# Delta-rule attention with a causal mixture on one core: small products on four array places, masks on other engines, a new order

## The chip, the cores and the metric

The kernel runs on one core of a Trainium2 chip. The metric is the device time of one execution in microseconds; the median of three runs stands for the kernel. TensorE (PE) multiplies, VectorE (DVE), ScalarE (ACT) and GpSimd (POOL) do the rest (POOL works on SBUF alone here), and all loads and stores are issued on SyncE's queue (SP).

## What is computed

The first half is linear attention with a delta rule over 4 batches, 8 heads, 768 tokens and 48 features; the second half is causal attention with four experts of 64 features, mixed by a top-2 gate.

```python
for t in range(S):
    y[:, :, t] = einsum('bhd,bhde->bhe', q[:, :, t], state)
    v_old = einsum('bhde,bhd->bhe', state, k_n[:, :, t])
    state = state + b[:, :, t] * einsum('bhd,bhe->bhde', k_n[:, :, t], v[:, :, t] - v_old)
x = y.transpose(0, 2, 1, 3).reshape(B, S, H * D)
for e in range(E):
    q, k, v = x @ wq[e], x @ wk[e], x @ wv[e]
    a = softmax(causal(q @ k.T / 8))
    out += gate[e] * (a @ v @ wo[e])
```

## The kernel before, in words

The work is cut into six units (`n`): two batches and 256 tokens each, that is 16 sequences of (batch, head), kept as 8 pairs (`p`) of two (`f`). A unit has four chunks (`c`) of 64 tokens. The features of sequence f lie on partitions 0 to 47 or 64 to 111 (`feat(f)`); its tokens lie on the opposite half (`tok(f)`), so a product from features to tokens uses one off-diagonal corner of TensorE's array for f = 0 and the other for f = 1.

Per chunk: `ga` forms k k^T and `gp` k q^T (16 small products each, two instructions a product); `pm` masks the latter on DVE. Then the state passes through: `ks` (state times keys), `xs` (v minus that, DVE), `tx` (times the solved triangular matrix in GF), `us` (copies, DVE and ACT), `ku` (adds to the state in PSUM bank 0), `se` (copies the state back), and `yy` gives the outputs; `yh`, `yl` and the small DMAs `hx` bring them into the layout of the second half, split in a high and a low part.

```python
def ga(n, c):
    g, k = slots(("ga", n, c), NP, 64), KF[zi(n, c) % RK]
    for p in range(NP):
        for f in range(2):
            mm(g[tok(f), p], k[feat(f), p], k[feat(f), p])
```

Once per unit the triangular system is solved for all 32 (chunk, pair): `bi` transposes on DVE, `nm` takes the norms by Newton steps, `sv.0` to `sv.32` eliminate in 32 steps (`sv.1` to `sv.30` are two POOL instructions each, one behind the other; `sv.31` is a selection on POOL), `bo` and `tn` transpose back on DVE, and `m1`, `we`, `m2`, `me` combine the two 32-token halves. Unit 0 has a solve of its own: `s0` on DVE in steps of 16 tokens, then `p1`, `w1`, `p2`, `w2`. POOL also scales v (`vs`) when its tile has landed.

The second half of a unit: `pj` and `pv` project, `kh`, `kl`, `ve` copy; `mx` forms scores for the row maximum, with a mask added by two bf16 products at the end; `mr` reduces on DVE; `mt`, `mo` turn the maximum; `sc` forms the scores again, transposed, in two banks; `sm` adds the mask there on DVE; `ex` takes the exponential on ACT; `av` multiplies with v on 128 rows and two column halves; `oe`, `ra`, `rb`, `nr` normalise (the last on POOL), `ft`, `oh`, `ol`, `fo`, `oo`, `so` project and store. `gt` is the gate.

PSUM has eight banks; bank 0 holds the state. The order of all 1711 steps is written out by hand as a string, ORDER: each word is a step with its numbers, and what stands behind @ is the bank, or the banks, of its result. Each engine executes its instructions in that order. `fl.31@2` issues 31 filler products of zeros, 128 columns each, whose result nobody reads.

Of the kernel before, what the change touches and what calls it, by code (L numbers as in the profile page):

```python
# [20 lines left out]
NEG = -1.0e9  # L21
RK, RQ, RV, RA = 8, 5, 3, 3
# [8 lines left out]
pm.0.0.1 ga.0.1@5 am.2 ae.3.2 ae.3.1 ae.3.0 ae.3.3 sq.1 al.3.3 ae.1.1 fl.3@6 gp.0.3@1 ae.1.2 ae.1.3 am.3 ae.1.0 sr.1
al.1.3 ga.1.0@2 am.1 pm.0.3.1 al.3.1 al.1.1 pm.0.3.0 gp.1.0@3 ge.1.0 bi.0 gp.0.1@1 sq.3 sq.2 fl.7@6 gp.0.2@2 sr.3 sr.2
ga.1.2@4 nm.0.0 nm.0.1 ga.1.1@5 ge.1.2 nm.0.2 wh.0 ge.1.1 nm.0.3 fl.10@6 ga.1.3@4 nm.0.4 ci bs ge.1.3 s0.1 s0.2 gd.1
s0.3 ww.1 s0.4 s0.5 s0.6 s0.7 s0.8 s0.9 s0.10 s0.11 s0.12 s0.13 s0.14 s0.15 wh.1 bi.1 wl.0 vs.0.1 ww.2 nm.1.0 vs.0.0
tn.0 wl.1 wh.2 bo.0 vs.0.2 ww.3 wl.2 nm.1.1 fl.208@6 p1.0@4 zz.3 ww.4 p1.3@5 nm.1.2 wh.3 wl.3 p1.1@6 w1.0 nm.1.3 wh.4
p1.2@4 wl.4 ww.5 p2.0@7 w1.1 w1.2 nm.1.4 ww.6 p2.2@4 sv.1.0 wh.5 p2.1@6 wl.5 w2.0.0 w2.2.0 wh.6 w2.0.1 tc0.0.1 w1.3
tc0.0.0 sv.1.1 w2.0.2 tc0.2.0 m1.0.2@5 sv.1.2 w2.2.2 tc0.2.1 m1.0.0@7 sv.1.3 w2.1.0 we.0.2 pm.0.2.0 sv.1.4 tc0.1.0
p2.3@5 pm.1.0.1 tc0.1.1 cl.0.0.1 we.0.0 cl.0.0.0 pm.1.0.0 sv.1.5 m2.0.0@7 pm.0.1.0 sv.1.6 m1.0.1@3 w2.3.1 me.0.0.0
w2.3.2 me.0.0.1 cl.0.1.0 w2.3.0 we.0.1 sv.1.7 tx.0.0@7 pm.0.1.1 tc0.3.1 tc0.3.0 w2.2.1 sv.1.8 m1.0.3@3 lv.0.3 us.0.0.0
us.0.0.1 ga.2.0@1 we.0.3 w2.1.2 sv.1.9 w2.1.1 ku.0.0 pm.0.2.1 ge.2.0 sv.1.10 yy.0.0@3 se.0.0.1 lt.0.3 se.0.0.0  # L40
m2.0.1@1 lq.1.1 sv.1.11 yh.0.0.0 ks.0.1@2 me.0.1.0 yl.0.0.0 me.0.1.1 cl.0.1.1 m2.0.2@4 yh.0.0.1 xs.0.1 lk.2.1 sv.1.12
m2.0.3@1 me.0.2.0 yl.0.0.1 lv.1.0 tx.0.1@5 me.0.2.1 me.0.3.0 sv.1.13 me.0.3.1 gp.1.1@4 us.0.1.0 us.0.1.1 cl.0.2.0
ku.0.1 pm.1.1.0 cl.0.3.1 sv.1.14 yy.0.1@1 pm.1.1.1 se.0.1.0 lt.1.0 se.0.1.1 ga.2.1@2 cl.0.2.1 lq.1.2 yh.0.1.0 sv.1.15
yh.0.1.1 ks.0.2@3 yl.0.1.0 ge.2.1 yl.0.1.1 cl.0.3.0 hx.0.0 xs.0.2 sv.1.16 lk.2.2 fl.11@7 tx.0.2@1 lv.1.1 sv.1.17
gp.1.2@2 us.0.2.1 us.0.2.0 yy.0.2@1 sv.1.18 pm.1.2.1 pm.1.2.0 ku.0.2 yh.0.2.0 lq.1.3 sv.1.19 ga.2.2@3 yl.0.2.0
se.0.2.0 lt.1.1 se.0.2.1 sv.1.20 pj.0.3.0.0@2 ge.2.2 pj.0.1.0.0@4 yh.0.2.1 pj.0.1.0.1 sv.1.21 pj.0.0.0.0@3 yl.0.2.1
pj.0.2.0.0@5 pj.0.3.0.1 ks.0.3@1 vs.0.3 sv.1.22 pj.0.2.0.1 xs.0.3 lk.2.3 pv.0.0.1@6 lv.1.2 sv.1.23 pj.0.0.0.1 ve.0.0.1
# [24 lines left out]
nm.3.4 oh.0.0 m1.2.1@4 kh.1.3.2 ol.0.0 me.2.0.0 pj.1.2.2.2 cz.2 kl.1.3.2 we.2.1 pv.1.1.0@7 kh.1.2.2 sv.3.0 m2.2.1@3
ve.1.1.0 lg.1.1.0 kl.1.2.2 sv.3.1 mx.1.0.1.1@45 sv.3.2 me.2.1.1 pm.3.0.0 fo.0.0.1@6 sv.3.3 me.2.1.0 pm.3.0.1 sv.3.4
# [761 lines left out]
```

## Time and profile before

| | |
|---|---|
| median of three runs (lowest, highest) | 489.33 us (488.55, 490.82) |
| profiled execution, span | 490.0 us |
| PE busy | 468.3 us, 96% |
| DVE, ACT, POOL busy | 282.3, 196.1, 217.7 us (58%, 40%, 44%) |
| instructions | 22373, of them 10076 products |
| filler products (zb) | 432, 29.2 us busy |
| HBM read, written | 21.92 MB, 4.72 MB |

Busy time of TensorE counts from the start of a product to its modelled end, and products overlap; so 96% does not say that the array is full. Two things are better guides: the distance from one block's start to the next one's start, and the idle time with what ended it. The profiled execution takes its time from the first to the last instruction; the runs' times stand 0.7 us lower at the median.

### The profile page before, as it was taken

To read this page: it belongs to the slowest core of one execution; us is meant where nothing else is said; L and a number is where in the kernel's file an instruction comes from. 1 tells how busy PE (TensorE), PEld (TensorE's weight loads), DVE (VectorE), ACT (ScalarE), POOL (GpSimd) and SP (SyncE) were. 2 spreads that over 40 slices of the span, in tenths; PEclk is the share of its full clock that TensorE was granted. 3 is DMA by queue.
4 is the path that set the end of the run, shared out by engine and by line. 5 is a ranking of instruction groups with operands and counts; after the bars stand their busy time and mean duration, and the time that the engine had idled before them with its cause. 6 is when DMAs were issued, how large, how long until landed. Compare 5 with 4: busy or idle time off the path is not lost.

```text
span 490.0 us, 22373 instructions
## 1 busy us (share of the span) xinstructions
PE 468.3 (96%) x10076; PEld 412.6 (84%) x10076; DVE 282.3 (58%) x561; ACT 196.1 (40%) x393; POOL 217.7 (44%) x416
## 2 busy tenths in 40 slices
PE   9995799899999999998999999999999999999997
PEld 8895698798889888887888899988988778877896
DVE  3899544195665777639457787414862375148511
ACT  4231244133445154444353344533545344442553
POOL 3243378812888248860386832897300110011111
PEclk9588559899999999999799999999999999999999
DMA  8832023342332523333113343201422011000101
GB/s 210 246 70 67 4 54 87 104 103 51 103 85 74 103 50 101 82 92 78 24 50 94 111 107 65 52 18 43 112 58 66 3 50 35 17 1 33 35 3 66
DMA packets 52863, 34.37 MB, mean 70 GB/s; under 512 B 34816, under 2 KB 46848, under 8 KB 52768
## 3 DMA queue, kind: packets, MB, share of 16 engines
q1 hardware_dynamic: 52768, 32.95, 25.8%
q8 instruction: 79, 1.29, 1.2%
q14 instruction: 16, 0.13, 0.1%
HBM read 21.92 MB, written 4.72 MB: 54 GB/s over the span
## 4 chain that ended last, share of the span: by engine, by line
PE 85%; DVE 8%; issue 3%; DMA 2%; ACT 1%; SPq 1%; ACTq 0%
PE p L183 82%; PE p L749 1%; DVE tm L404 1%; DVE vs L406 1%; DMA kf<-in_kq_dram 1%; PE p L675 1%; DVE tn L415 1%; DMA xu<-h 1%; SPq L575 1%; DVE b L471 1%; DVE qp L334 1%; DVE at L342 1%; DVE gf L412 0%; DMA qp<-in_kq_dram 0%; DVE ss L363 0%
## 5 line engine op out<-in xcount | busy, mean ns | idle before, releaser
L465 POOL TENSOR_TENSOR tm<-b 128x30 f32<-128x30 f32 (+9 forms) x150 | 72.8, 485 | 34.5 <-DVE rs L736 14.3
L467 POOL TENSOR_TENSOR b<-b,tm 128x30 f32<-128x30 f32 (+9 forms) x150 | 77.7, 518 | 11.8
L711 ACT ACTIVATE at<-p 128x768 f32<-128x768 f32 (+1 forms) x48 | 43.4, 916 | 34.7 <-PE p L183 21.5
L185 ACT ACTIVATE z<-p 48x384 f32<-48x384 f32 (+1 forms) x68 | 33.0, 486 | 45.5 <-PE p L183 40.7
L666 DVE TENSOR_REDUCE mp<-p 128x2 f32<-128x1024 f32 (+3 forms) x40 | 44.2, 1115 | 11.1 <-PE p L183 10.6
L183 PE MATMUL p<-vs,at 128*64 128x65 f32 x1344 | 47.2, 224 | 0.6 <-issue 0.6
L183 PEld LDWEIGHTS p<-vs,at 128*64 128x64 f32 x1344 | 42.3, 137 | 6.4 <-issue 3.4
L511 POOL TENSOR_TENSOR kv<-kv,nt 128x384 f32<-128x384 f32 x24 | 19.8, 831 | 60.8 <-DMA kv<-in_kv_dram 60.8
L183 PE MATMUL p<-xu,wh 128*128 128x512 f32 (+1 forms) x168 | 43.6, 399 | 0.3 <-DMA xu<-h 0.3
L334 DVE TENSOR_TENSOR qp<-p,cs 64x512 f32<-64x512 f32 x48 | 32.9, 688 | 8.6 <-PE p L183 7.9
L183 PEld LDWEIGHTS p<-xu,wh 128*128 128x128 f32 x168 | 30.1, 209 | 6.8 <-DMA xu<-h 0.5
L742 POOL TENSOR_TENSOR rs<-rs,gw 128x8 f32<-128x8 f32 x12 | 3.3, 278 | 71.8 <-DVE rs L739 71.6
L183 PE MATMUL p<-kf 48*64 48x64 f32 x768 | 31.6, 243 | 2.5 <-DMA kf<-in_kq_dram 2.5
L183 PE MATMUL p<-qp,kf 48*64 48x64 f32 x768 | 30.7, 232 | 2.7 <-issue 1.0
L183 PEld LDWEIGHTS p<-kf 48*64 48x64 f32 x768 | 28.7, 156 | 5.4 <-DMA kf<-in_kq_dram 2.7
L183 PEld LDWEIGHTS p<-qp,kf 48*64 48x64 f32 x768 | 27.4, 146 | 4.9 <-issue 2.2
L183 PE MATMUL p<-qh,kh 64*128 64x128 f32 (+1 forms) x192 | 30.9, 318 | 0.0
L183 PE MATMUL p<-zb 128*128 128x128 bf16 x432 | 29.2, 229 | 1.1 <-DVE zb L298 1.1
L533 DVE COPY z<-p 64x384 f32<-64x384 f32 x24 | 13.5, 561 | 26.5 <-ACT z L185 21.4
L183 PEld LDWEIGHTS <-zb 128*128 128x128 bf16 x432 | 26.6, 103 | 2.0 <-DVE zb L298 1.1
L183 PE MATMUL p<-qp,z 128*48 128x64 f32 (+1 forms) x768 | 27.2, 225 | 0.0
L183 PE MATMUL p<-qh,kl 64*128 64x128 f32 (+1 forms) x192 | 27.1, 278 | 0.0
(143 smaller groups left out, 991.0 us busy)
## 6 DMA issues: line engine op xcount, KB each, us to landing
kv<-in_kv_dram SPq DMA_DIRECT2D x46, 192.0 KB, 2.8
kf<-in_kq_dram SPq DMA_DIRECT2D x24, 224.0 KB, 3.1
out_dram<-ot SPq DMA_DIRECT2D x24, 192.0 KB, 2.3
qp<-in_kq_dram SPq DMA_DIRECT2D x38, 96.0 KB, 2.4
gf<-gf SPq DMA_DIRECT2D x20, 128.0 KB, 2.9
xu<-h SPq DMA_DIRECT2D x72, 32.0 KB, 2.1
qp<-in_kq_dram SPq DMA_DIRECT2D x10, 128.0 KB, 5.7
gf<-zr SPq DMA_DIRECT2D x10, 128.0 KB, 3.2
```

The costliest lines, as they stand in the source:

```text
L183: T.matmul(o, lhsT=a, rhs=b, start=start, stop=True, skip_group_check=True)
L185: copy = lambda o, a: S.activation(o, a, AF.Copy)
L334: V.tensor_tensor(QP[zi(n, c) % RQ][r, f], slots(("gp", n, c), NP, 64)[r], PMK[r, None, :].to_broadcast([64, NP, 64]), op=OP.mult)
L342: V.tensor_copy(o, a)
L404: V.tensor_tensor(tv, BX[:, :, i:i + 1, i + 1:].to_broadcast([128, 2, i, m]), BX[:, :, 0:i, i:i + 1].to_broadcast([128, 2, i, m]), op=OP.mult)
L406: V.tensor_tensor(BX[:, :, 0:i, i + 1:], BX[:, :, 0:i, i + 1:], tv, op=OP.add)
L465: G.tensor_tensor(tv, B2[:, i:i + 1, i + 1:].to_broadcast([128, i, m]), B2[:, 0:i, i:i + 1].to_broadcast([128, i, m]), op=OP.mult)
L467: G.tensor_tensor(B2[:, 0:i, i + 1:], B2[:, 0:i, i + 1:], tv, op=OP.add)
L511: G.tensor_tensor(vt, vt, NRM[n % 2][:, c * NP:c * NP + NP, None].to_broadcast([128, NP, HD]), op=OP.mult)
L533: V.tensor_copy(o, a)
L666: V.tensor_reduce(o[:, :, y0:y0 + per], g, axis=AX.X, op=OP.max, negate=True)
L711: S.activation(at(n, b, y, kp)[:, :, 0:w], P8[:, b0:b0 + 2, 0:w], AF.Exp, scale=0.125)
```

## The change

The step `l3` and the bf16 mask tiles go. Every odd pair of units 1 to 5 now keeps its tokens on the same half as its features (`rows`), and even pairs as before; the host lays out v and beta accordingly. `ga`, `ks` and `tx` then go round the four corners of the array, and where ORDER gives them two neighbouring banks (20 of 24 `ga`, 19 of 22 `ks`, 20 of 24 `tx`) even pairs write the one and odd pairs the other (`duo`). The mask of `mx` becomes a DVE addition in PSUM (`mk`, 32 of them) between `mx` and `mr`; `sm` becomes a selection on POOL behind `ex`. There are six instead of five buffers for q, four instead of three for k and v by token, five instead of three for the exponentials, which ORDER now assigns. Filler products have 512 columns; there are 51 of them instead of 432. ORDER is new throughout.

```diff
-RK, RQ, RV, RA = 8, 5, 3, 3
+RK, RQ, RV, RA = 8, 6, 4, 5
-zb zz.2 lk.0.2 lk.0.0 lt.0.0 lq.0.0 lc.0 ex0 lk.0.3 lk.0.1 lt.0.1 zz.1 lq.0.3 lk.1.0 lq.1.0 lq.0.1 l3 lt.0.2 lq.0.2
+zb fl.1@1 fl.1@2 fl.1@3 fl.1@4 fl.1@5 fl.1@6 fl.1@7 lt.0.1 sq.1 lt.0.3 sq.3 lt.0.2 sr.1 lt.0.0 lk.0.3 sq.2 sr.2 sq.0
...
+def rows(n, p, f):
+    g = f if n and p % 2 else 1 - f
+    return slice(64 * g, 64 * g + 64)
...
+    def two(key, w):
+        a, b = BK[key]
+        return P8[:, a:b + 1, 0:w]
...
+    def duo(key, w):
+        b = BK[key]
+        if len(b) == 1:
+            return slots(key, NP, w).rearrange("p (k t) w -> p k t w", t=2)
+        return two(key, 4 * w).rearrange("p t (k w) -> p k t w", w=w)
...
-    ZB = sb("zb", 128, dt=BF16)
-    IB = sb("ib", 128, dt=BF16)
-    MB = sb("mb", 128, dt=BF16)
+    ZB = sb("zb", 512, dt=BF16)
...
-            mm(P8[:, BK["fl", k][0], 0:128], ZB, ZB)
+            mm(P8[:, BK["fl", k][0]], ZB[:, 0:128], ZB)
...
-        g, k = slots(("ga", n, c), NP, 64), KF[zi(n, c) % RK]
+        g, k = duo(("ga", n, c), 64), KF[zi(n, c) % RK]
         for p in range(NP):
             for f in range(2):
-                mm(g[tok(f), p], k[feat(f), p], k[feat(f), p])
+                mm(g[rows(n, p, f), p // 2, p % 2], k[feat(f), p], k[feat(f), p])
...
-                mm(g[tok(f), p], k[feat(f), p], z[feat(f), f, p])
+                mm(g[rows(n, p, f), p // 2, p % 2], k[feat(f), p], z[feat(f), f, p])
...
-                mm(g[tok(f), p], GF[n % 2][tok(f), NP * c + p], x[tok(f), p])
+                mm(g[tok(f), p // 2, p % 2], GF[n % 2][rows(n, p, f), NP * c + p], x[rows(n, p, f), p])
...
-        if k0 + nb == 2 * (n % 3) + i + 1:
-            for x in range(2):
-                mm(g[:, x, :, 128 * nb - 128:], IB, MB[:, None, :].to_broadcast([128, per, 128]), False)
+
+    def mk(n, b, i, r):
+        k0, nb, y0, per, sec, g = mv(n, b, i, r)
+        V.tensor_tensor(g[:, :, :, 128 * nb - 128:], g[:, :, :, 128 * nb - 128:], KM[:, None, None, :].to_broadcast([128, 2, per, 128]),
+                        op=OP.add)
...
-        b0 = BK["sc", n, b, y, n % 3][0]
-        g = P8[:, b0:b0 + 2, 0:256].rearrange("p x (j q) -> p x j q", j=2)
-        V.tensor_tensor(g, g, KM[:, None, None, :].to_broadcast([128, 2, 2, 128]), op=OP.add)
+        a = at(n, b, y, n % 3)[:, :, 0:256].rearrange("p x (j q) -> p x j q", j=2)
+        G.affine_select(a, a, pattern=[[0, 2], [0, 2], [1, 128]], compare_op=OP.is_ge, fill=0.0, base=0, channel_multiplier=-1)
```

The first place is the start on DVE, around the transposition of unit 0's matrix (`vs<-tn`) and the scaling that follows (`vs<-vs,aa`, two instructions). Before, up to the first Newton step (the other thirteen norm instructions, up to aa, stand behind these, and then the scaling):

```order
L334 TENSOR_TENSOR qp_75<-p_63,cs 64x512 x2
L392 STREAM_TRANSPOSE vs<-tn 128x1024
L363 TENSOR_REDUCE ss_86<-vs 128x8 x2
L371 TENSOR_SCALAR g_87<-ss_86 128x32
L372 TENSOR_SCALAR g_87<-g_87 128x32
L374 RECIPROCAL rr_88<-g_87 128x32
```

And now:

```order
L357 COPY at_111<-p_63 32x256
L396 TENSOR_SCALAR nt_98<-g_89 128x32
L397 TENSOR_TENSOR rr_90<-nt_98 128x32
L398 RECIPROCAL rr_90<-rr_90 128x32
L399 STREAM_TRANSPOSE nn_91<-rr_90 128x32
L400 TENSOR_TENSOR aa_92<-nn_91,bt 128x32
L404 STREAM_TRANSPOSE vs<-tn 128x1024
L409 SCALAR_TENSOR_TENSOR vs<-vs,aa_92 128x16x16 x2
```

The sums (ss) and the whole norm moved ahead of the transposition, and the masking of q (qp) went away from the copies.

The second place is DVE behind the small solve of unit 0, where `gf<-vs` is the transposition that releases p1 on PE, `b<-gf` unit 1's first, and `tn<-vs` the one that p2 needs. Before:

```order
L408 TENSOR_TENSOR vs<-vs,aa_90 128x2x16x16
L409 COPY vs<-aa_90 128x32
L392 STREAM_TRANSPOSE b<-gf_81 128x1024
L370 COPY ss_91<-b 128x32
L371 TENSOR_SCALAR g_92<-ss_91 128x32
L372 TENSOR_SCALAR g_92<-g_92 128x32
L415 STREAM_TRANSPOSE tn<-vs 128x32x32
L412 STREAM_TRANSPOSE gf_80<-vs 128x32x32
```

And now:

```order
L420 TENSOR_TENSOR vs<-vs,aa_92 128x2x16x16
L421 COPY vs<-aa_92 128x32
L424 STREAM_TRANSPOSE gf_82<-vs 128x32x32
L404 STREAM_TRANSPOSE b<-gf_83 128x1024
L427 STREAM_TRANSPOSE tn<-vs 128x32x32
L382 COPY ss_93<-b 128x32
```

The releasing transposition moved from the third of three to the first.

The third place is POOL inside the solve of unit 3, where `tm<-b` and `b<-b,tm` are the solve's steps, `at` holds exponentials, and rs and os are a normalisation. Now:

```order
L479 TENSOR_TENSOR b<-b,tm 128x18x13
L720 AFFINE_SELECT at_111<-at_111 128x2x256
L746 TENSOR_TENSOR rs_119<-rs_119,gw_132 128x8
L747 TENSOR_TENSOR os_117<-os_117,rs_119 128x512
L477 TENSOR_TENSOR tm<-b 128x228
L479 TENSOR_TENSOR b<-b,tm 128x19x12
```

A selection and a normalisation stand in the queue between two steps of the solve; before, no selection of exponentials stood on POOL at all.

## Rows read from the trace of the kernel before

**Rows 1.** Page, chain of waits: shares of the span by line.
```profile
PE p L183 82%; PE p L749 1%; DVE tm L404 1%; DVE vs L406 1%; DMA kf<-in_kq_dram 1%; PE p L675 1%; DVE tn L415 1%; DMA xu<-h 1%; SPq L575 1%; DVE b L471 1%; DVE qp L334 1%; DVE at L342 1%; DVE gf L412 0%; DMA qp<-in_kq_dram 0%; DVE ss L363 0%
```

**Rows 2.** Windows: stretch, length, busy us (instructions) of PE, PEld, DVE, ACT, POOL; clock, DMA.
```profile
0.00:62.97 62.97, 51.64 (x1447) 49.08 (x1447) 46.26 (x105) 18.34 (x44) 23.02 (x42) 0.75 0.43 116
62.97:490.10 427.13, 416.66 (x8630) 363.48 (x8630) 236.00 (x457) 177.77 (x350) 194.65 (x375) 0.98 0.25 63
```

**Rows 3.** The same windows for the filler tile zb alone, without POOL.
```profile
0.00:62.97 62.97, 18.13 (x262) 16.83 (x262) 0.11 (x1) 0.20 (x1) 0.75 0.43 116
62.97:490.10 427.13, 11.03 (x170) 9.76 (x170) 0.00 (x0) 0.00 (x0) 0.98 0.25 63
```

**Rows 4.** Timeline, TensorE: start, us, line, operation, tiles, shapes, count [idle before].
```profile
42.29 1.75 PE L183 MATMUL p<-gf,at 32*32 32x32 f32 x182 [2.29 <-DVE gf L412]
...
150.53 0.28 PE L183 MATMUL p<-qh,kl 64*128 64x256 f32 x2
150.65 0.28 PE L183 MATMUL p<-mr,sl 64*128 64x256 f32 x2
150.86 1.14 PE L183 MATMUL p<-x,gf 64*64 64x48 f32 x32
151.93 0.63 PE L183 MATMUL p<-wh,xu 128*128 128x260 f32 x3
152.39 0.52 PE L183 MATMUL p<-wl,xu 128*128 128x260 f32 x3
...
153.20 0.92 PE L183 MATMUL p<-vs,at 128*64 128x65 f32 x24
...
155.84 1.57 PE L183 MATMUL p<-vs,at 128*64 128x65 f32 x48
157.34 1.15 PE L183 MATMUL p<-kf 48*64 48x64 f32 x32
158.32 1.09 PE L183 MATMUL p<-z,kf 48*64 48x48 f32 x32
```

**Rows 5.** Timeline, TensorE, around two pairs of mask products.
```profile
134.71 0.39 PE L183 MATMUL p<-mb,ib 128*128 128x256 bf16 x2
135.03 1.13 PE L183 MATMUL p<-z,kf 48*64 48x48 f32 x32
...
185.57 0.28 PE L183 MATMUL p<-mb,ib 128*128 128x128 bf16 x2
185.70 0.61 PE L749 MATMUL p<-cs,os 128*128 128x128 f32 x4
```

**Rows 6.** Timeline, VectorE in the start; last row TensorE, first state product.
```profile
16.11 1.95 DVE L392 STREAM_TRANSPOSE vs<-tn 128x1024 f32<-128x1024 f32 x1
...
23.24 0.76 DVE L397 SCALAR_TENSOR_TENSOR vs<-vs,aa 128x256 f32<-128x256 f32 x2
...
34.50 1.28 DVE L409 COPY vs<-aa 128x32 f32<-128x32 f32 x1
...
40.05 2.10 DVE L412 STREAM_TRANSPOSE gf<-vs 128x1024 f32<-128x1024 f32 x1
...
45.27 0.42 DVE L428 TENSOR_TENSOR at<-p,w 128x256 f32<-128x256 f32 x1
...
62.97 1.95 PE L183 MATMUL p<-kv,gf 64*64 64x48 f32 x32 [0.33 <-ACT gf L498]
```

**Rows 7.** Timeline: POOL in unit 2, first m1 blocks of units 1 and 5.
```profile
119.71 0.24 POOL L465 TENSOR_TENSOR tm<-b 128x30 f32<-128x30 f32 x1
...
155.92 1.27 POOL L469 TENSOR_SCALAR_AFFINE_SELECT b<-b 128x1024 f32<-128x1024 f32 x1
...
107.21 1.20 PE L183 MATMUL p<-gf 32*32 32x32 f32 x64
...
348.19 1.20 PE L183 MATMUL p<-gf 32*32 32x32 f32 x64
```

**Rows 8.** Groups by line, VectorE: count, busy us, mean ns; idle before.
```profile
L716 DVE TENSOR_TENSOR p<-p,km 128x512 f32<-128x512 f32 x24 | 16.8, 699 | 17.0 <-PE p L183 16.9
```

More of the change, by code (lines that the diff above doesn't have):

```diff
@@ L31 @@
[L31 to L35, printed above, removed]
@@ L649, in mv @@
         k0, nb, y0, per, sec = rounds(n, i)[r]
[L650 to L651 removed]
+        return k0, nb, y0, per, sec, two(("mx", n, b, i, r), 128 * nb * per).rearrange("p x (y k) -> p x y k", y=per)
     def mx(n, b, i, r):
@@ L678, in mo @@
         copy(MR[b], bank(("mt", n, b), 256))
-    SEQ = {}
-    for n_ in range(NU):
-        for b_ in range(2):
-            for y_ in range(2):
-                for k_ in range(n_ % 3 + 1):
-                    SEQ[n_, b_, y_, k_] = len(SEQ)
     def at(*a):
-        return AT[SEQ[a] % RA]
+        return AT[BK["ex", *a][0]]
     def cells(n, kp):
@@ L696, in sc @@
     def sc(n, b, y, kp):
-        b0 = BK["sc", n, b, y, kp][0]
+        g = two(("sc", n, b, y, kp), 512)
         for j, (kb, o, q0) in enumerate(cells(n, kp)):
@@ L789, in _layout, with turn @@
     feat_ = lambda x: x.transpose(0, 4, 5, 3, 8, 1, 2, 6, 7).reshape(NU, CH, 2, HD, 1, NP * 64)
-    tok_ = lambda x: x[:, :, :, ::-1].transpose(0, 4, 5, 3, 6, 7, 1, 2, 8).reshape(NU, CH, 128, 1, NP * HD)
+    def turn(x):
+        y = x[:, :, :, ::-1].copy()
+        y[:, :, 1::2] = x[:, :, 1::2]
+        y[0][:, :, :, 0] = x[0][:, :, ::-1, 0]
+        return y
+    tok_ = lambda x: x.transpose(0, 4, 5, 3, 6, 7, 1, 2, 8).reshape(NU, CH, 128, 1, NP * HD)
     kq = np.zeros((NU, CH, 2, 64, 2 * NP * 64), np.float32)
@@ L793, in _layout @@
     a = {"kq": kq.reshape(NU, CH, 128, -1),
[L794 to L796 removed]
+         "kv": np.concatenate([tok_(k[:, :, :, ::-1]), tok_(turn(v))], 3).reshape(NU, CH, 128, -1)}
+    a["beta"] = turn(b).transpose(3, 6, 5, 1, 2, 0, 4, 7, 8).reshape(128, NU * 32)
+    order = []
     for t in range(3):
         for x in range(2):
[L799 to L800 removed]
+            order += list(range(96 * t + 48 * x, 96 * t + 48 * x + 48))
+            order += list(range(288 + 48 * x + 16 * t, 288 + 48 * x + 16 * t + 16))
     ww = lambda n: np.asarray(inputs["moe_" + n])
     cat = lambda w: w.transpose(1, 0, 2).reshape(DM, NE * EH)
[L803 removed]
+    f = lambda w: w[order].reshape(3, 128, -1).transpose(1, 0, 2).reshape(128, -1)
     a["wqk"] = f(np.concatenate([cat(ww("wq")), cat(ww("wk"))], 1))
@@ L817, in _layout @@
     c[:, 624:656] = ((i % 32) < 16)[:, None] & (j >= 16)[None, :]
-    c[:, 752:880] = np.where(i[:, None] > i[None, :], NEG, 0.0)
     a["consts"] = c
```

315 lines of the change are left out of this document (155 added, 160 removed).

## The prediction

> **What bounds the kernel now.** First the chain of waits: 82% of the span lies on one line, the helper in which every product is issued [rows 1]. TensorE therefore comes first, and the question is where it works and where it only waits. The table of two stretches, cut where the first state product of unit 0 starts (62.97 us, tx.0.0 [rows 6]), answers it [rows 2]. Behind the cut TensorE is busy 416.66 of 427.13 us at a granted clock of 0.98; ahead of it the clock is 0.75, and of its 51.64 busy us 18.13 are filler products that compute nothing [rows 2, 3]. So there are two regimes: up to 63 us a serial chain on VectorE, then 427 us in which a microsecond less on TensorE is a microsecond less on the clock, unless another engine turns out to be late. Behind the cut fillers take 11.03 us more [rows 3]. My sum is made against the profiled execution (span 490.0 us; the median of three runs is 489.33, 0.7 lower). About 0.5%, 2.4 us, is what a measurement of this kernel can tell from no change.
>
> **Part 1, four places instead of two.** A small block (ga, ks, tx) is 16 products of at most 64x64, each two instructions, 32 in all. They alternate between two corners of the array. From its start to the next block's, tx takes 151.93 - 150.86 = 1.07 us and ga 158.32 - 157.34 = 0.98 us [rows 4]; ks, listed at 158.32 with 1.09 us against ga's 1.15, I take like ga. How much of this is fixed is read from another block on two places: 24 instructions of av are listed with 0.92 us, 48 with 1.57, and from the start of the 48 to the next block it is 1.50 (155.84 to 157.34) [rows 4]. So 24 more cost 0.65 us, 54 ns a pair, and of the 1.50 us 0.20 are fixed. Of a 1.0 us block 16 pairs at 54 ns are 0.86 us; in groups of four it is 8 rounds, so 0.43 us go.
>
> Can four run at once? Two halves of it stand in the trace. av's two places share all rows of the array and differ in the columns, and 54 ns a pair is the rate above. The score products use two row halves with all columns and write two banks: a pair of 256 columns goes by in 0.12 us (150.53 to 150.65), where three products of 260 columns on the whole array, one after the other, take 0.46 (151.93 to 152.39), 0.15 each [rows 4]. Four corners with two banks are the two together. The instruction rate is no limit either: in p1, which goes round four diagonal corners of 32x32, 182 instructions take 1.75 us, 9.6 ns each [rows 4], while the new blocks need one in 13.5 ns. The Trainium skill says otherwise ("TensorE: Matmul & The Clock Gate", section "Wait — 56ns, not 53.3ns?"): "Start-to-start never drops below ≈25 ns however small N is". By that rule 32 instructions would need 0.80 us, only some 0.06 us would go in a block, and the sum below would end near 470. The trace does not agree, with 9.6 ns.
>
> Blocks with two banks: 20 ga, 20 tx and 19 ks (unit 0 stays on two corners for ga and tx, and its ks have one bank). Four of the ga are unit 1's, and they now run in the start, where TensorE waits anyway; 55 count. 55 x 0.43 = **23.7 us**. Ends: 0, if nothing more overlaps, and 59 x 0.5 = 29.5, if the fixed part halves too.
>
> **Part 2, masks.** 32 pairs of mask products leave TensorE. The narrow pair stands 0.13 us ahead of the next work (185.57 to 185.70), the wide one 0.32 us (134.71 to 135.03) [rows 5]; 16 of each make 7.2 us. Part of that distance may remain with whatever work comes next; I take **6 us**, between 3 and 8. In exchange VectorE gets 32 additions in PSUM of 256 or 512 columns, and loses 24 of 512 columns at 699 ns [rows 8], so its load stays within 4 us either way, on an engine that is busy 236 of 427 us [rows 2]. But each addition stands between the products and the row maximum. Products of other steps stand there in the order, so I cost the wait at nothing; without that cover it is 0.4 to 0.7 us in 32 places, 18 us at worst. The other mask goes to POOL, behind the exponential: 24 selections on 128x512. POOL has a selection of twice that size at 1.27 us [rows 7]; I take 0.65, with 0.3 and 1.27 as ends, 16 us in all on an engine busy 195 of 427 us [rows 2].
>
> **Part 3, the start.** On VectorE the transposition for unit 0 starts at 16.11 and ends at 18.06; the sums and the norm then fill it up to 23.24 [rows 6]. In the new order sums and norm stand ahead of that transposition, made possible by loading the token-side tiles first: 5.2 us go. Next, the copy that ends the small solve starts at 34.50 and takes 1.28 us, and the transposition that releases p1 starts at 40.05, because two others and unit 1's first norm steps are ahead [rows 6]. It is now directly behind: 4.3 us go. The first transposition itself may start some 2.5 us sooner, since masking products for q no longer interrupt the copies; this is the loosest of the three, between -2 (feature tiles are now fifth to eighth in the load queue) and 4. So p1 starts at 42.3 - 12 = 30.3. Behind it, though, VectorE now first does the two transpositions that it put off (2.0 and 1.9 us) and 2.3 us of norm, so that the first masked copy comes 6.2 us behind the release instead of 3.1: at about 36.5 against 45.27 [rows 6]. From there to tx.0.0 it was 17.7 us; counting the VectorE rows that stand there now gives some 8.2 us, and products, copies and the three fillers behind them 3.5 more. tx.0.0 then starts near 48.4 instead of 62.97, 14.6 us sooner. Four blocks that ran ahead of it now run after it (two gp, a p2, an m1, about 4.3 us), so the gain is **10.3 us**; ends 3 and 15.
>
> **Part 4, more buffers and fewer fillers.** Fewer filler products behind the cut give back nothing by themselves: they stood where TensorE waited. I leave the waits there as they are (10.5 us idle, 11.0 filled [rows 2, 3]); with six query buffers and four token buffers some may go, 7 us at most by my choice. Copies from two banks read the same number of columns: nothing. The last product blocks now wait for a selection on POOL behind the exponential, 1 us more at the end, against one fewer on the path before it: nothing.
>
> **Sum:** 490.0 - 23.7 - 6 - 10.3 = 450.0 us of span; less the 0.7 by which the median stands lower, **449 us**. With the good ends: 490 - 29.5 - 8 - 15 would be 437, less a few of the waits 434. With masks 3, start 3 and the middle of part 1: 460.
>
> **Rivals.**
> *The solve on POOL becomes the bound.* Each unit's solve is a chain that runs from one unit's first m1 to the next one's: for unit 2 POOL's first step comes 12.5 us behind unit 1's m1 (107.21 to 119.71), its last ends 37.5 us later at 157.19, and about 5 us of transpositions follow on VectorE, 2 us each as in [rows 6]: 55 us [rows 7]. Four such cycles (107.21 to 348.19) took 241 us, 60 each, in which TensorE was the bound [rows 7]. The change takes some 48 blocks x 0.43 = 20.6 us and 5 of masks out of them, so TensorE needs about 215, 54 a unit. POOL now also has selections in the queue between the solve's steps. If the cycle grows to 57 with them, 3 us a unit are lost, 12 us in all: 461 us. Against it: the 12.5 us contain a wait of POOL for a token tile, for which there are now four buffers.
> *Four places give no more than two* (the pairs collide, or issue is the limit): part 1 is 0, and the time 449 + 24 = 473. Against it speak the three rates above.
> *Slower: POOL's queue stands still behind the selections.* POOL takes its instructions in order, and about 12 of the 24 selections stand ahead of the last step of the last solve. Each waits for an exponential, which waits for scores. If every one held the queue for 5 us, the solves would move by 60 us and 490 be passed: 449 + 60 less about 12 us of slack in the cycles is 497. It decides from some 4.4 us each. For it speaks only that the waits of this kind are unknown; against it, that scores and exponentials stand well ahead of most selections in the order.
>
> **How the numbers follow.** Forecast 0.60; POOL's cycle 0.20; two places 0.09; slower 0.05; the rest, 0.06, mixtures such as a late start with exposed mask additions: 455 to 468 for half, near 489 for the other. The range from 434 to 468 holds the forecast, POOL's cycle and half of the mixtures, 0.83, and leaves out 473, 489 and 497. Faster by over 0.5%: 0.60 + 0.20 + 0.09 + 0.03 = 0.92; same 0.03; slower 0.05.
>
> **What would show it.** Right: tx.0.0 starts between 45 and 52 us; ga, ks and tx from unit 1 on take 0.55 to 0.65 us from start to next start; VectorE's span from the first transposition to the scaling has no gap; TensorE is busy over 95% behind tx.0.0. Wrong: such blocks still near 1.0 us (two places); m1 of units 2 to 5 preceded by idle or filler time with the last solve step on POOL as releaser (POOL's cycle); waits of POOL for ScalarE in front of selections adding up to tens of us (slower); a tx.0.0 later than 58 us, which would make part 3 wrong.

## The result, and the profile after

The changed kernel takes **436.6 us** (median of 434.8, 435.6, 437.6 and 442.5) against 489.9 us for the kernel before on the same chip: a ratio of 0.891, interval 0.887 to 0.895. The run of 442.5 us is in the chip's slower state and is left out of the ratio. The forecast was 449 us, the range 434 to 468. Direction and range held; the point was 12 us too high, and the terms behind it were off by more than their sum, as the runs below show. The profiled execution took 434.8 us, 433.1 of them span. The two profiled executions lie 56.9 us apart in span, 3.6 us more than the medians, so differences read from this one pair of traces are uncertain by a few us in all.

The page of the changed kernel: busy time, the selections on POOL, the instruction queue, the chain of waits by line.

```profile
PE 398.9 (92%) x9626; PEld 354.2 (82%) x9631; DVE 279.9 (65%) x569; ACT 187.8 (43%) x391; POOL 235.2 (54%) x440
...
q8 instruction: 75, 1.23, 1.2%
...
PE p L190 63%; POOL b L479 4%; POOL tm L477 3%; DMA xu<-h 3%; SPq L587 2%; DMA kf<-in_kq_dram 2%; DMA qp<-in_kq_dram 1%; DVE tn L427 1%; DVE tm L416 1%; PE p L753 1%; DVE vs L418 1%; DVE b L404 1%; DVE b L483 1%; DVE gf L424 1%; DVE b L473 1%
...
L720 POOL TENSOR_SCALAR_AFFINE_SELECT at<-at 128x512 f32<-128x512 f32 x24 | 16.5, 694 | 25.1 <-ACT at L716 25.1
```

The windows, cut at the first state product as in [rows 2], and the same for the filler tile as in [rows 3] (here without POOL too):

```profile
0.00:54.69 54.69, 37.58 (x1037) 28.10 (x1040) 39.55 (x96) 13.74 (x33) 24.10 (x47) 0.77 0.53 136
54.69:433.10 378.41, 361.35 (x8591) 326.10 (x8592) 240.34 (x474) 174.04 (x358) 211.09 (x394) 0.97 0.27 70
...
0.00:54.69 54.69, 12.57 (x44) 4.54 (x47) 0.27 (x1) 0.00 (x0) 0.77 0.53 136
54.69:433.10 378.41, 0.83 (x3) 0.31 (x4) 0.00 (x0) 0.21 (x1) 0.97 0.27 70
```

The cut moved from 62.97 to 54.69 us, 8.3 sooner instead of the 14.6 forecast. Behind it 427.1 us became 378.4, 48.7 fewer where 25.4 were forecast. Of these TensorE's filler time gave 10.2 (11.03 to 0.83), its other work 45.1 (405.6 to 360.5), and its idle time grew by 6.6 (10.5 to 17.1). TensorE is busy 95.5% behind the cut, as the prediction's signs asked (over 95%); tx.0.0 at 54.69 lies outside their 45 to 52 us, though not beyond the 58 that would have made part 3 wrong.

The start (timeline; VectorE, then POOL, then TensorE), to be held against [rows 6]:

```profile
18.14 1.96 DVE L404 STREAM_TRANSPOSE vs<-tn 128x1024 f32<-128x1024 f32 x1
...
20.13 0.76 DVE L409 SCALAR_TENSOR_TENSOR vs<-vs,aa 128x256 f32<-128x256 f32 x2
...
31.04 1.31 DVE L421 COPY vs<-aa 128x32 f32<-128x32 f32 x1
...
32.38 2.20 DVE L424 STREAM_TRANSPOSE gf<-vs 128x1024 f32<-128x1024 f32 x1
...
40.37 0.42 DVE L440 TENSOR_TENSOR at<-p,w 128x256 f32<-128x256 f32 x1
...
31.03 1.26 POOL L309 TENSOR_TENSOR wl<-at,wh 128x512 fp32r<-128x512 f32 x1 [2.88 <-ACT wh L192]
...
54.69 1.95 PE L190 MATMUL p<-kv,gf 64*64 64x48 f32 x32
```

What TensorE waited for behind the cut (in total, times, longest):

```profile
PE p L190 <- issue: 4.8, 9, 1.3
PE p L190 <- DMA xu<-h: 3.9, 9, 1.4
PE p L190 <- DVE x L532: 2.1, 3, 1.5
```

In the programs of the experiments the same steps stand a few lines lower or higher. The changed kernel was also run again on the chip of the start's experiments (`changed_again`, below); its block distances are used from here on.

A table worked out from the timelines, TensorE only, from tx.0.0 to the last product: for each kind of block the sum of the distances from its start to the next block's start, less the idle time inside, in us, with the number of blocks (before / after where they differ). "changed" is the second run; `two_places` and `order_alone` are experiments of the next section.

```
blocks       number     before  changed  two_places  order_alone
ga, ks, tx   62          65.5     40.5      63.6        63.9
mx           48          26.2     16.0      15.6        25.2
sc           48          52.7     47.3      47.3        47.4
av           48          44.7     41.7      42.0        41.9
pj           84          59.7     57.3      59.5        56.9
m1, m2       24 / 25     25.8     27.0      26.0        26.5
others       137 / 140  131.8    132.6     130.2       130.5
fillers      9 / 2       10.3      1.2       1.2         1.2
idle                      7.1     14.1       8.4         6.7
sum                     423.8    377.7     393.8       400.2
```

Two rows are as forecast in kind: ga, ks and tx lose 25 us (forecast 23.7), mx 10 (forecast 6). The surprise is that sc, av and pj lose 10.8 as well, although nothing in them was changed, and that fillers lose 9. The 2.4 us of pj are the least certain part: over the profiles with this order, in which pj is the same, it takes 56.6 to 59.9 us.

### The profile page after: what moved, and what is told of

It reads as the page before. It is cut to its first block, busy times and chain, and to the rows that moved or that the text cites. A ratio compares the mean times of both kernels' runs of the same rounds, so it can differ in the third digit from the quotient of the medians.

```text
span 433.1 us, 21448 instructions
## 1 busy us (share of the span) xinstructions
PE 398.9 (92%) x9626; PEld 354.2 (82%) x9631; DVE 279.9 (65%) x569; ACT 187.8 (43%) x391; POOL 235.2 (54%) x440
## 3 DMA queue, kind: packets, MB, share of 16 engines
q8 instruction: 75, 1.23, 1.2%
## 4 chain that ended last, share of the span: by engine, by line
PE 65%; DVE 11%; POOL 7%; DMA 6%; issue 4%; SPq 3%; ACT 2%; ACTq 0%; DVEq 0%; POOLq 0%
PE p L190 63%; POOL b L479 4%; POOL tm L477 3%; DMA xu<-h 3%; SPq L587 2%; DMA kf<-in_kq_dram 2%; DMA qp<-in_kq_dram 1%; DVE tn L427 1%; DVE tm L416 1%; PE p L753 1%; DVE vs L418 1%; DVE b L404 1%; DVE b L483 1%; DVE gf L424 1%; DVE b L473 1%
## 5 line engine op out<-in xcount | busy, mean ns | idle before, releaser
L477 POOL TENSOR_TENSOR tm<-b 128x30 f32<-128x30 f32 (+9 forms) x150 | 72.7, 485 | 44.9 <-DVE b L473 34.1
L716 ACT ACTIVATE at<-p 128x768 f32<-128x768 f32 (+1 forms) x48 | 43.0, 917 | 25.4 <-PE p L190 25.0
L190 PE MATMUL p<-vs,at 128*64 128x65 f32 x1344 | 43.4, 223 | 0.0
L190 PEld LDWEIGHTS p<-vs,at 128*64 128x64 f32 x1344 | 40.9, 137 | 2.8 <-issue 2.1
L720 POOL TENSOR_SCALAR_AFFINE_SELECT at<-at 128x512 f32<-128x512 f32 x24 | 16.5, 694 | 25.1 <-ACT at L716 25.1
L190 PE MATMUL p<-qh,kh 64*128 64x128 f32 (+1 forms) x192 | 28.3, 292 | 0.2 <-DVE h L579 0.2
L532 DVE TENSOR_TENSOR x<-kv,p 128x384 f32<-128x384 f32 x22 | 12.2, 553 | 24.4 <-PE p L190 21.0
L190 PE MATMUL p<-qp,kf 48*64 48x64 f32 x768 | 27.5, 223 | 0.0
L190 PE MATMUL p<-mr,sl 64*128 64x128 f32 (+1 forms) x192 | 27.0, 277 | 0.0
L190 PE MATMUL p<-ql,kh 64*128 64x128 f32 (+1 forms) x192 | 26.9, 277 | 0.0
L190 PE MATMUL p<-wh,xu 128*128 128x260 f32 x144 | 26.2, 293 | 0.6 <-DMA xu<-h 0.6
L190 PEld LDWEIGHTS p<-qp,z 128*48 128x48 f32 (+1 forms) x768 | 24.2, 127 | 1.5 <-DVE z L545 0.4
L190 PEld LDWEIGHTS p<-qp,kf 48*64 48x64 f32 x768 | 25.1, 138 | 0.4
L545 DVE COPY z<-p 64x384 f32<-64x384 f32 x24 | 13.4, 560 | 15.5 <-PE p L190 9.8
```

Of the source, the lines that this page charges most:

```text
L190: T.matmul(o, lhsT=a, rhs=b, start=start, stop=True, skip_group_check=True)
L477: G.tensor_tensor(tv, B2[:, i:i + 1, i + 1:].to_broadcast([128, i, m]), B2[:, 0:i, i:i + 1].to_broadcast([128, i, m]), op=OP.mult)
L532: V.tensor_tensor(split(X), split(KV[zi(n, c) % RV][:, 1]), duo(("ks", n, c), HD), op=OP.subtract)
L545: V.tensor_copy(o, a)
L716: S.activation(at(n, b, y, kp)[:, :, 0:w], two(("sc", n, b, y, kp), w), AF.Exp, scale=0.125)
L720: G.affine_select(a, a, pattern=[[0, 2], [0, 2], [1, 128]], compare_op=OP.is_ge, fill=0.0, base=0, channel_multiplier=-1)
```

## Experiments

**What the four places are worth: `two_places`.**

```diff
 def rows(n, p, f):
-    g = f if n and p % 2 else 1 - f
-    return slice(64 * g, 64 * g + 64)
+    return slice(64 - 64 * f, 128 - 64 * f)
```

> The changed kernel with its small products ga, ks and tx back on two corners of the array (rows() gives the opposite half for every pair, v and beta are laid out to match); bank pairs, masks, order and buffers stay. Four places worth what the block distances say: ga, ks and tx blocks return to about 1.05 us each from start to start, 55 of them give back 23 to 25 us, and the time is 458 to 462. Rival, that most of the gain came from the new order and that a longer block would partly fill waits that the changed kernel has anyway: under 450.

Measured: 451.7 us, ratio 0.925 (0.921 to 0.930). Against the changed kernel (0.891 and 0.896 in two comparisons) that is about 0.032 of 489 us, **16 us**, with an uncertainty of some 3: between the two expectations. The blocks themselves did what the theory said. The state's tx and the two ga blocks that follow in the timeline, in the changed kernel (second run):

```profile
180.21 0.68 PE L190 MATMUL p<-x,gf 64*64 64x48 f32 x32
180.83 0.66 PE L753 MATMUL p<-cs,os 128*128 128x128 f32 x4
...
186.97 1.16 PE L190 MATMUL p<-kf 48*64 48x64 f32 x64
188.06 0.39 PE L190 MATMUL p<-qh,kh 64*128 64x256 f32 x2
...
189.10 0.22 PE L190 MATMUL p<-qh,kh 64*128 64x128 f32 x2
...
190.02 0.22 PE L190 MATMUL p<-qh,kh 64*128 64x128 f32 x2
...
190.94 0.28 PE L190 MATMUL p<-qh,kh 64*128 64x256 f32 x2
```

and in `two_places`:

```profile
187.53 1.14 PE L189 MATMUL p<-x,gf 64*64 64x48 f32 x32
188.60 0.66 PE L752 MATMUL p<-cs,os 128*128 128x128 f32 x4
...
194.61 2.08 PE L189 MATMUL p<-kf 48*64 48x64 f32 x64
196.62 0.39 PE L189 MATMUL p<-qh,kh 64*128 64x256 f32 x2
```

and what TensorE waits for there:

```profile
PE p L189 <- DVE x L531: 1.1, 3, 0.5
PE p L189 <- DMA xu<-h: 1.0, 3, 0.6
```

tx goes from 1.07 to 0.62 us, two ga from 2.01 to 1.09. In the table the three kinds lose 23.1 us. But TensorE's idle time rises from 8.4 to 14.1: the waits for the small transfers of hx (xu<-h) go from 1.0 to 3.9 us in the first profile of the changed kernel and 3.4 in the second, those for xs on VectorE (x) from 1.1 to 2.1 and 1.5. So 5.7 of the 21.8 us that TensorE's work lost in all between these two came back as waits, half of them or more in the chain of the state and in the transfers behind it; the rest is spread over single waits.

**The masks: `mask_products`.**

```diff
 def mx(n, b, i, r):
...
+        if k0 + nb == 2 * (n % 3) + i + 1:
+            for x in range(2):
+                mm(g[:, x, :, 128 * nb - 128:], IB, MB[:, None, :].to_broadcast([128, per, 128]), False)
...
 def mk(n, b, i, r):
-    V.tensor_tensor(...)
+    pass
```

> The changed kernel with the row-maximum mask back on TensorE, 32 pairs of bf16 products behind the mx products, and without the 32 additions on VectorE. By the block distances of the two traces the masked mx blocks return from 11.8 to some 20 us, so the time grows by 8 to 9 us, to 444. If the additions on VectorE cost waits that now go, or TensorE's waits swallow the products: growth under 4 us.

Measured: 442.9 us, ratio 0.908 (0.904 to 0.913), some 7 us more than without; the mx blocks take 25.5 us instead of 16.0. That is nearer the theory (8 to 9) than the rival (under 4). TensorE's idle time is 13.5 us with the products and 14.1 with the additions, so no waits for the additions show.

**The order alone: `order_alone`**, both edits together.

> Both of the former at once: two corners and mask products, with the new order, banks and buffers kept. If the parts add up: 436 + 24 + 8.5 = 468 to 469, so that the order, with the buffers, is worth the other 20 us against the kernel before. If they overlap (one covers waits of the other): under 463; if the new order is good only with the short blocks: over 475.

Measured: 458.1 us, ratio 0.940 (0.936 to 0.944). The two parts overlap a little (451.7 + 6.4). The finding is what remains: with two places and mask products, so with next to the same work on TensorE, the new order, banks and buffers take **30 us** off the 488.0 us that the kernel before took there. (What else of the change stays in this run, the selection on POOL, the longer filler products and a setting of the DMA scratch size, is in these 30 us too; no run tells the order from the buffers.) By the profiles (490.0 and 456.7 us of span) these are 9.8 in the start (tx.0.0 at 53.2), 9.1 of filler time, 14.1 of other work on TensorE and 0.4 of idle time. The 14.1 are the question: 10.9 of them stand in the table at sc, av and pj, in which nothing was changed. The clock is not the answer: behind tx.0.0 the granted clock is 0.50 for 19.4 us in the kernel before and for 23.4 us in `order_alone`.

**Fillers between like blocks and unlike: `split_like` and `split_same`.** Counted in the two orders from tx.0.0 on, the number of places where TensorE's next block uses the array in another shape (all of it, row halves, column halves, corners, 32-row squares) fell from 307 to 181. sc now follows sc 27 times (11 before), av follows av 28 times (12).

```diff
+        if name == "sc" and last == "sc":
+            mm(P8[:, BK[("sc", *a)][0], 0:128], ZB[:, 0:128], ZB[:, 0:128])
```

> The changed kernel with one filler product of 128x128 by 128 columns ahead of each of the 27 sc blocks that follow another sc block (the filler writes the bank that the sc block then overwrites). Theory, that a change of the array's shape (rows by columns in use) costs 0.1 us or so each time, and that the new order gains some 13 us by 126 fewer such changes: each filler makes two changes where there was none, so the distance from one sc to the next grows from 0.93 by 0.2 to 0.3 us, and the time by 5 to 8 us. Rival, that only the columns count and the order gained by fewer waits: 0.06 us each, under 2 us in all.

`split_same` has the same product ahead of 46 pj, pv and fo blocks behind blocks on the whole array:

> The counterpart to the run with fillers between sc blocks: the same filler product (128x128, 128 columns) ahead of 46 pj, pv and fo blocks that follow a block on the full array, so that the shape in use does not change. Theory (a change of shape costs, the filler alone does not): the block behind it starts 0.05 to 0.08 us later, 46 times, 2.5 to 4 us in all, against the 0.36 us each that the fillers between sc blocks took. Rival (any extra product with its own bank costs some 0.3 us, by its wait or its switch of bank): 0.3 us each, 14 us.

Measured: `split_like` 444.4 us, ratio 0.913 (0.908 to 0.917), some 9 us more for 27 products. Timeline:

```profile
188.53 0.39 PE L191 MATMUL p<-qh,kh 64*128 64x256 f32 x2 [0.18 <-DVE h L580]
...
189.46 0.28 PE L191 MATMUL p<-mr,sl 64*128 64x256 f32 x2
189.67 0.23 PE L191 MATMUL p<-zb 128*128 128x128 bf16 x1
189.83 0.33 PE L191 MATMUL p<-qh,kh 64*128 64x128 f32 x2
...
190.94 0.23 PE L191 MATMUL p<-zb 128*128 128x128 bf16 x1
191.10 0.33 PE L191 MATMUL p<-qh,kh 64*128 64x128 f32 x2
```

These are the same blocks as at 188.06 to 190.94 in the changed kernel above: 189.10 to 190.02 was 0.92 us from sc to sc, 189.83 to 191.10 is 1.27. From the filler to the sc behind it are 0.16 us. Over all 27 the distances grow from 26.0 to 34.1 us, 0.30 each. In `split_same` the same product costs next to nothing:

```profile
199.79 0.23 PE L191 MATMUL p<-zb 128*128 128x128 bf16 x1
199.83 0.94 PE L191 MATMUL p<-xu,wh 128*128 128x512 f32 x3
...
200.61 0.23 PE L191 MATMUL p<-zb 128*128 128x128 bf16 x1
200.65 0.61 PE L191 MATMUL p<-wh,xu 128*128 128x260 f32 x3
```

0.04 us from filler to block; the 46 distances grow from 38.8 to 40.9 us, 0.05 each (0.07 without the idle time inside). So of the 0.30 some 0.25 are two changes of shape, **0.12 us each**, measured for a change from row halves to the whole array and back. If other changes cost the same, 126 fewer are 15 us, and 14.1 were found. The traces bear this out for the other shapes on average: in `before`, `order_alone` and `changed_again` alike, a block whose next one has another shape lies 0.09 to 0.11 us further from it than a block of the same form whose next one has the same shape (some 430 distances without idle time in each), which makes 11 to 14 us. The total of `split_same`, 442.6 us (0.906, 0.900 to 0.912), is more than its 2.1 us explain: its interval reaches down to 441, and what the rest is stays open.

**GpSimd's queue: `no_selection`**, sm() left empty: the run leaves out the 24 selections.

> The changed kernel without the 24 selections on GpSimd behind the exponentials; the entries above the diagonal of the last block are then summed too, which this run leaves wrong in the output. In the changed kernel the selections take 16.5 us and GpSimd waits 25.1 us for the exponentials ahead of them, in the queue in which the solve steps stand. Theory, that the units' solve cycle is not what bounds (only one m1 waits for it, 1.0 us): time within 2.5 us of the changed kernel's. Rival, GpSimd's cycle bounds: 6 us or more faster.

Measured: 436.6 us, ratio 0.891 (0.886 to 0.896). No gain: 16.5 us of selections and 25.1 us of waiting for exponentials stood in time that POOL had to spare. The first m1 blocks of units 1 and 5 lie 214.3 us apart (93.8 to 308.1) where they lay 241.0 apart [rows 7], and 214.7 in this run, so the selections do not lengthen the cycle, and TensorE still sets it.

**The start.** `changed_again` is the changed kernel once more, the measure for three runs beside it:

> The changed kernel itself on this chip, as the measure for the three runs beside it: 434 to 437 us, its first state product tx.0.0 between 52 and 55 us.

Measured: 438.4 us, ratio 0.896 (0.890 to 0.902), tx.0.0 at 53.6.

`features_first` loads the feature tiles ahead of the token tiles:

```diff
-lt.0.1 sq.1 lt.0.3 sq.3 lt.0.2 sr.1 lt.0.0 lk.0.3 sq.2 sr.2 sq.0 sr.3 lk.0.1 ...
+lk.0.3 lk.0.1 lk.0.0 lk.0.2 lt.0.1 lt.0.3 lc.0 lt.0.2 lt.0.0 ...
```

> The changed kernel with the start's loads in the other order: feature tiles ahead of token tiles, and the copies out of ga ahead of the sums on VectorE; the norm stays ahead of the scaling. In the changed kernel TensorE waits for the feature tiles until 7.73 us, and its first four ga blocks take 1.6 us each. Theory, that this is why the first transposition came at 18.1 and not near 13.6: it now starts between 11 and 14, the scaling between 16.5 and 18.5 instead of 20.13, and the time falls by 1.5 to 4 us. Rival, that the order of the loads only swaps which of two chains is late, since the last of the eight tiles lands at the same time: scaling within 0.8 us of 20.1, time unchanged.

Measured: 440.0 us (0.899, 0.894 to 0.904), no gain. ga starts at 4.36 instead of 7.27, but the norm now waits for the sums, and the scaling stays at 20.01: the rival, two chains that change places. The edit did more than that: in this order POOL's weight copies and scalings of v run beside the small solve, which takes 13.8 us (20.01 to 33.78) instead of 11.2, and tx.0.0 comes at 56.6, 3 us later than in `changed_again`. So the unchanged time does not price the load order by itself.

```profile
17.98 1.99 DVE L406 STREAM_TRANSPOSE vs<-tn 128x1024 f32<-128x1024 f32 x1
20.01 0.76 DVE L411 SCALAR_TENSOR_TENSOR vs<-vs,aa 128x256 f32<-128x256 f32 x2
```

`w1_first` puts `w1.1 w1.0` ahead of `nm.1.0`, and `gp.0.0` behind `p2.0`:

> The changed kernel with the first two masked copies w1.1 and w1.0 ahead of unit 1's norm on VectorE, and one gp block behind p2.0 instead of ahead of p2.1. In the changed kernel the norm stands between p1's end and w1.0 (43.74 us). Theory, that the chain on VectorE sets tx.0.0: it starts 1.5 to 2.5 us sooner and the time falls by as much. Rival 1, TensorE sets it, at a granted clock of 0.50 there: under 0.7 us sooner. Rival 2, unit 1's solve on POOL, which starts about 1 us later, takes the gain back: tx.0.0 sooner, time unchanged.

Measured: 439.7 us (0.897, 0.891 to 0.903), no gain, tx.0.0 at 54.8. This edit was badly built: a masking step that needs the moved gp block held VectorE 2.65 us ahead of 45.90. It tells nothing of the theory.

`filled_start` has `fl.56` in place of `fl.21`:

> The changed kernel with 56 filler products of 512 columns instead of 21 while the small solve runs, so that TensorE works until p1 comes (it is idle from 26.7 to 34.6 us in the changed kernel, and its granted clock is 0.50 from 30 to 60 us). Theory, that half the clock behind the small solve costs the start some us: p1's 192 products take 1.9 instead of 2.8 us, and tx.0.0 comes 1 to 3 us sooner. Rival, VectorE's chain sets tx.0.0 whatever the clock: under 0.5 us.

Measured: 443.1 us (0.905, 0.899 to 0.910), some 5 us slower than `changed_again`, though the intervals just overlap. The clock column shows 1.00 from 30 to 40 us, and p1's first 192 instructions take 1.87 us instead of 2.78; yet tx.0.0 comes at 53.9. TensorE now stands still three times without anything to wait for:

```profile
38.50 0.79 PE L192 MATMUL p<-qp,kf 48*64 48x64 f32 x19 [1.76 <-issue]
...
42.34 0.48 PE L192 MATMUL p<-at,tn 32*32 32x32 f32 x18 [1.94 <-issue]
...
46.33 0.74 PE L192 MATMUL p<-tn,at 32*32 32x32 f32 x20 [1.44 <-issue]
```

Each of these ends 2.3 to 2.7 us after a packet of the instruction queue q8 (at 36.01, 39.63 and 44.06). The fillers also ran about 1 us beyond the point where p1 could have begun, and behind the cut this run took 6.5 us more than `changed_again`. Part of that may be the clock: the granted clock is 0.50 for 34.5 us behind the cut here, and for 24.6 us in `changed_again`; whether the fillers brought that about is not shown.

`quick_start` shortens the start in three places: 14 of the 16 copies `ae` on ACT with the norm on VectorE ahead of them, six more `fl.1`, and no two-input operation of POOL beside the small solve (`wh.0 wl.0` ahead of `bi.0`, `vs.0.3` behind `wl.1`).

```diff
 def ae(c, q):
...
-        if q % 2:
+        if c == 2 and q % 2:
             V.tensor_copy(o, a)
```

> The changed kernel with a start made shorter in three ways: 14 of the 16 copies out of the first ga blocks on ScalarE, so that VectorE does the norm meanwhile; 6 more fillers ahead of the first ga block, so that TensorE does not stand still before it; and the weight copy wh.0, wl.0 ahead of the small solve, one scaling of v behind it, so that no two-input GpSimd operation runs beside the solve (in the changed kernel single solve steps of 0.25 us took 0.9 and 1.3 us exactly while one did). Theory: ga blocks 1.0 instead of 1.6 us, first transposition at 14 to 15.5 instead of 17.4 to 18.1, solve 9.5 instead of 11.2 us, p1 at 27.5 to 30 and tx.0.0 4 to 5 us sooner; the time falls by 3 to 5 us. Rival, what follows p1 (TensorE at half clock and short of instructions, unit 1's loads) takes it back: tx.0.0 under 2 us sooner, time within 1.5 us.

Measured: 435.8 us, ratio 0.887 (0.881 to 0.892); span 429.5 us in the profiled execution, the fastest of them, tx.0.0 at 50.5. What the third place removes, first in the changed kernel (second run; VectorE, then POOL):

```profile
21.67 0.25 DVE L416 TENSOR_TENSOR tm<-vs 128x88 f32<-128x88 f32 x1
21.95 1.34 DVE L418 TENSOR_TENSOR vs<-vs,tm 128x88 f32<-128x88 f32 x1
...
21.91 1.27 POOL L309 TENSOR_TENSOR wl<-at,wh 128x512 fp32r<-128x512 f32 x1 [5.33 <-ACT wh L192]
```

then in `quick_start` the same step, and the solve's two ends:

```profile
18.56 0.76 DVE L411 SCALAR_TENSOR_TENSOR vs<-vs,aa 128x256 f32<-128x256 f32 x2
...
21.12 0.25 DVE L420 TENSOR_TENSOR vs<-vs,tm 128x88 f32<-128x88 f32 x1
...
28.08 2.19 DVE L426 STREAM_TRANSPOSE gf<-vs 128x1024 f32<-128x1024 f32 x1
```

A step of 0.25 us takes 1.34 us where POOL's operation begins just ahead of it, and ends 0.1 us behind that operation; without it the solve takes 9.5 us (18.56 to 28.08) instead of 11.2, as expected. The ga blocks stayed at 1.4 us (four in 5.50), so the transposition came at 16.5, not 14 to 15.5. tx.0.0 is 3 us sooner than in `changed_again`; in the time 0.887 against 0.891 and 0.896 is not told apart from no gain, since the intervals overlap.

`quick_start_w1` adds `w1.1 w1.0` ahead of `nm.1.0`, with gp.0.0 where it was.

> The run with the shorter start, and in addition the masked copies w1.1 and w1.0 ahead of unit 1's norm on VectorE, this time with the gp block left where it was (in the earlier run it stood behind p2.0, and a masking step that waits for it then held VectorE 2.65 us). In the run without this, TensorE waits 2.79 and 1.43 us for w1.1 and w1.0. Theory: these waits fall to under 1 us together, tx.0.0 starts at 47.5 to 49 instead of 50.5, and the time falls by 1.5 to 3 us against that run, to a ratio near 0.881. Rival 1, instructions: TensorE runs out of them instead (idle that waits for nothing in the profile) and tx.0.0 stays within 0.7 us. Rival 2, unit 1's solve on GpSimd starts some 0.8 us later and takes the gain back by the first m1 of unit 1.

Measured: 434.5 us, ratio 0.888 (0.883 to 0.892), tx.0.0 at 50.7. Rival 1: the waits for w1 are gone, and in their place stands

```profile
39.21 0.47 PE L192 MATMUL p<-tn,at 32*32 32x32 f32 x17 [2.41 <-issue]
```

This run and `quick_start` are the quickest versions seen, by a margin over the changed kernel that these runs do not resolve.

## Why the prediction was right, and where its steps failed

*What bounds.* Right: TensorE behind the cut (361 of 378 us busy), a chain on VectorE ahead of it.

*Part 1, four places, 23.7 us.* Right for the blocks: the 0.57 us (ga) and 0.64 (tx) that the forecast comes to for one are 0.54 (two ga in 1.09) and 0.62, and 23.1 us went. The rule of the Trainium skill cited there ("TensorE: Matmul & The Clock Gate", section "Wait — 56ns, not 53.3ns?"), no less than about 25 ns from start to start, would give 0.80 us a block; the trace does not agree, though the last section shows where 25 ns do come up. What failed is the sentence that a microsecond less on TensorE is one less on the clock: 16 us of the 23 arrived, and idle time took 5.7. The prediction had made the exception of another engine that is late, but put it at nothing. The prediction looked at what TensorE did, and not at how far the transfers and copies of the state's chain were from being late. Its sentence that the instruction rate is no limit was drawn from a burst (182 instructions in 1.75 us), and the next row of the same trace, which it did not show, has TensorE standing still behind that burst with nothing to wait for:

```profile
46.01 1.22 PE L183 MATMUL p<-gf,at 32*32 32x32 f32 x73 [1.97 <-issue]
```

*Part 2, masks, 6 us.* Right in kind and in size: 6.4 to 7 us in time, 9.5 in the blocks, whose upper end I had put at 8. The waits that the additions might have exposed did not come. A selection takes 0.694 us where 0.65 was estimated.

*Part 3, the start.* 8.3 instead of 14.6 us. Of its three sub-terms the norm ahead of the transposition held (scaling 2.0 us behind its start, 7.1 before) and the transposition directly behind the solve held (32.38, straight after the copy). The third, the one called loosest, came out at its bad end, -2.0 instead of 2.5: the feature tiles land behind the token tiles, the first ga runs at 7.3 to 7.7, and VectorE then has the sums, the norm and eight copies to do, with little idle time between them (0.40 and 0.70 us). `features_first` shows that the loads alone were not the cause; in `quick_start`, where most copies left VectorE, the norm ended 4.5 us sooner than in `changed_again`, but the transposition only 0.9 us sooner, since it then waited for POOL's masking. A price inside the term was also taken wrong, though without harm, since it stood in both kernels: the "copy of 1.28 us" that ends the solve takes 0.20 in the second run, and is long only where POOL's wl begins beside it (31.03). The Trainium skill says why ("SBUF — State Buffer", section "SBUF: two separate sides"): VectorE and GpSimd share one pair of ports, "an exclusive lock, not a bandwidth split", which the one that starts first holds for its whole instruction. The solve step of 1.34 us, which starts 0.04 us behind POOL's operation of 1.27 us and ends 0.1 us behind its end, agrees. The last stretch, from w1 to tx.0.0, took 14.3 us where 8.2 + 3.5 were counted: I counted VectorE's rows and 3.5 us for the rest, where TensorE is busy 10.2 us of the 14.3, at a granted clock of 0.50, and stands still 2.0 us more under "issue". How much each of these costs is not shown: with the clock at 1.00 up to 40 us `filled_start` got no earlier tx.0.0.

*Part 4, waits left as they are.* The step that failed most by its sign: filler time fell by 10.2 us and did not come back as idle time while blocks were long (`order_alone`: 6.7 idle, 1.2 filled, against 7.1 and 10.3). "7 us at most by my choice" was a number without a row behind it. Whether the order or the buffers removed these waits is open.

*The missing term.* The largest error is one that no part names: the order puts like blocks together, 126 fewer changes of the array's shape, 11 to 15 us by the distances, 14 found. The rows to see it by were there. In the kernel before, sc is followed by another sc in 0.92 to 1.05 us, and by anything else mostly in 1.11 to 1.16 (9 of 37 in 1.01 to 1.05); the prediction took every block at its mean and asked only which blocks went.

So the sum came within 12 us because errors met: the start 6 too much, four places 8 too much in time, masks about right, and against them 9 us of filler time and 14 us of changes that were not forecast. That the time lies in the range, 2.6 us above its lower end, is luck in this sense: none of the stated good ends is what brought it there. The 0.7 us at the sum's end was no property of the kernel either, but the difference of two executions; in the runs on record the time is 1.7 us above the span of the same execution. By the runs the order and buffers gave 30 us of the 53, four places 16, masks 6 to 7.

*The rivals.* POOL's cycle as the bound (461 us) and the queue behind the selections (497) are refuted by `no_selection` and by the 214.3 us between the m1 blocks, 53.6 a unit where TensorE was put at 54 and the rival at 57; the marker named for the latter, waits of POOL for ScalarE of tens of us, did appear (25.1 us) and cost nothing, so it was a bad marker. Two places' worth (473) is refuted by the blocks.

## What to carry to other kernels

On TensorE price an order, not only a list of blocks: group the distances to the next start by what comes next, and count how often the shape in use changes between the two orders. A saving on the bounding engine is worth its full size only until the chain beside it is late; look for the waits that are just under zero before taking it in full. And before a duration is taken from a row, look whether another engine's operation begins and ends with it.

## What the runs showed of the hardware

- **A change of the array's shape costs about 0.12 us** between row halves and the whole array, an added product of 128 columns without one 0.05 (`split_like`, `split_same`); over all shapes in use it is 0.09 to 0.11 on average, by the distances in three traces.
- **TensorE can run out of instructions.** The page's q8 moved 1.23 MB in 75 packets for 19257 recorded products and weight loads, which is 64 bytes each and 256 to a packet. In the 14 profiles two such packets never start closer than 3.25 us: 12.7 ns an instruction, or 25 ns for a recorded product with its weight load, is the fastest supply seen. p1's 9.6 ns a product [rows 4] and the 17 ns of a four-place block (32 in 0.54 us) are faster than that, so by this reading they live from what was fetched before. In the start of `filled_start` a faster clock went with 5.1 us of idle time under "issue", against 1.8 in `changed_again`. That the packets are the cause is read from their times, not shown by an edit.
- **The clock column is no witness in the first microseconds.** The trace's first record of the clock stands at 6.0 us in `quick_start` and at 12.6 us in the changed kernel; ahead of it the column shows 1.00. In `quick_start` it shows 1.00 from 0 to 7 us, where 13 fillers of 512 columns take 5.29 us (0.41 each), and 1.00 again from 13.5 us on, where nine take 2.12 us (0.24 each). In the changed kernel it shows 1.00 up to 26 us, although the first four ga blocks take 6.1 us from 7.73 on, 1.5 each; for all but their last 1.3 us no clock is on record.
